# An attention block fused with a rational-function layer: second layer one tick later, another shifted unit, x requested behind its last reader

## The chip, the cores and the metric

One core of a Trainium2 chip runs the whole program. The metric is the device time of one execution in microseconds, less is better. The engines named here are TensorE (PE, with its weight loads as PEld), VectorE (DVE), ScalarE (ACT), GpSimd (POOL), and SyncE (SP), whose queue issues all the DMAs of this program.

## What is computed

`x` has 4 batches of 12480 rows of 128; `inducing` has 32 rows of 128. Cut to what matters:

```python
def mab(q, kv):
    s = scale * (q @ kv.transpose(0, 2, 1))
    a = np.exp(s - s.max(-1, keepdims=True))
    a /= a.sum(-1, keepdims=True) + 1e-09
    return a @ kv
h = mab(I, x)                 # 32 pooled rows of each batch
x2 = mab(x, h)                # each row of x attends to the 32 pooled rows
hh = x2.reshape(49920, 128) @ w_in            # 2048 columns
P = a[0] + a[1] * hh + a[2] * hh**2 + a[3] * hh**3
Q = 1.0 + abs(b[0]) * abs(hh) + abs(b[1]) * hh**2
out = (P / (Q + 1e-6)) @ w_out
```

## The kernel before

**Blocks, units, ticks.** The 49920 rows are cut into 104 blocks of 480 rows (26 per batch). For one block the 2048 hidden columns are worked on in 8 units of 256 (2 halves of 128). So there are 832 units, and `fast_ticks` (L894) writes the program tick by tick: in tick t unit t enters the first layer, and older units are at later stages. Ticks are only a way of writing; on the chip every engine runs its own list in order and waits by semaphores. With t counted from 0 and eight units to a block, the unit number within a block is the tick's number modulo 8, and ticks are named by it below (tick 5 is the tick in which a unit 5 enters).

**What a tick writes.** `first` (L838) for the unit of the next tick: two matmuls into a PSUM tile `hp` (three of them) from the attention weights `at` and the stack `st`. A *plain* unit then gets its absolute value by a bit mask on DVE (`mask`, `u<-hp`) and after that two more matmuls on PE that add a constant to `hp` (`moved`, L853, `hp<-same,by`), which may not start before the mask has read `hp`. A *shifted* unit (`shifted`, L778) has the constant in `st` already, gets its absolute value from ACT and needs neither mask nor `moved`. Units 1, 3 and 7 are shifted, and 0, 2, 4, 5, 6 plain. One tick later DVE forms `l` from `u` and `hp` (`l<-u,all,hp`). ACT turns `u` of pairs of units into a logarithm and later a sigmoid, four pairs at a time. BEHIND = 13 ticks after entering, in odd ticks, DVE finishes the even unit of a pair (`l<-l,all,u`) and POOL the odd one (`last_on_pool`, L952). `second` (L858) multiplies the finished unit with `w_out` into the one PSUM tile `po` of its block: four matmul instructions, two for each half. This happens 14 ticks after entering (`done`, L909), half of it ahead of `first` and half behind; for unit 7 two matmuls (`po<-at,st`) follow that close the block's sum.

**Where a block's result leaves.** `po` exists once. When unit 7 has been through `second`, the next call of `fetch` (L879) writes the copy `oT<-po` on DVE and the DMA of `oT` to the output. `side` (L789), which runs in every tick, calls it (L799), so the copy stands in the same tick behind `l`. The first `second` of the next block may not write `po` before that copy has read it; in its tick, called `late` (L912), `second` therefore stands at the tick's end. With 14 ticks unit 7's `second` falls in tick 5 and the late tick is tick 6.

**Attention beside it.** `side` also feeds the attention work of the next batch and block into the ticks, in small pieces, under a budget of DVE, POOL and PE time per tick (`SPARE`, L195). `pass1` (L375) multiplies x with `inducing` (`pc`, from tiles `xTa`), `pooled` (L446) the exponentials with x (`ph`, from tiles `x`), `pass3` (L651) x with the pooled rows (`pd`, from `xTb`); groups of four blocks of x each, tile by tile in four buffers of a kind. `landed` (L327) holds a group back until three ticks after the request of its fourth tile, where that request has been written already. `columns` (L333) requests tile n+4 when tile n+1 is taken; `pooled` requests tile n+3 at the first reading of tile n. Spreading a block's `at` onto partitions takes eight DMAs from SP per pair of blocks.

Every engine call goes through one helper, so nearly all instructions carry line 177 in the profile; they are told apart by tile names.

Of the kernel before, what the change touches and what calls it, by code (L numbers as in the profile page):

```python
# [21 lines left out]
M = 32  # L22
C = 128
HB = 4
BT = HB * TP
# [167 lines left out]
class Kernel:  # L193
# [138 lines left out]

    def columns(self, b, kind):  # L333

        ts = [self.x_columns(b, n, kind) for n in range(4)]

        def turns():
            for n in range(self.NB):
                yield ts.pop(0)
                if n + 4 < self.NB:  # L340
                    ts.append(self.x_columns(b, n + 4, kind))

        return turns()

    def wide_columns(self, b):

# [28 lines left out]
    def pass1(self, b):  # L375

        nc, ap = self.nc, self.ap
        X = mybir.AxisListType.X
        e = ap.tile([P, self.NG, BT], F32, tag="e", name=f"e{b}")
        mxs = ap.tile([P, self.NG, 2], F32, tag="mxs", name=f"mxs{b}")  # L380
        nc.gpsimd.memset(mxs, -3.0e38)
        xs = self.wide_columns(b) if self.boot else self.cols.pop((b, "a"))
        for g in range(self.NG):
            nb = min(4, self.NB - 4 * g)
            yield from self.landed("a", b, g)
            yield "pe", 1.0
            pc = self.misc(f"pc{b}_{g}")
            for j in range(nb):
                nc.tensor.matmul(pc[M * j:M * j + M, 0:BT], self.ind, next(xs), start=True, stop=True)
            rows = slice(0, M * nb)  # L390
            for i in range(2):
                yield "v", 0.36
                c = slice(BT // 2 * i, BT // 2 * (i + 1))
                nc.vector.tensor_scalar(out=e[rows, g, c], in0=pc[rows, c], scalar1=1.0, scalar2=None, op0=ALU.mult, op1=ALU.max, accum_out=mxs[rows, g, i:i + 1])
            self.free()
        if self.boot:
            self.wide_rows(b)
        else:
            self.xs[b] = [self.x_rows(b, n) for n in range(4)]
        yield "v", 0.1  # L400
        mx = ap.tile([P, 1], F32, tag="mx", name=f"mx{b}")
        nc.vector.tensor_reduce(out=mx, in_=mxs.rearrange("p g i -> p (g i)"), axis=X, op=ALU.max)
        yield "pe", 0.2
        pm = self.misc(f"pm{b}")
        nc.tensor.transpose(out=pm[0:1, 0:P], in_=mx, identity=self.ident)
        yield "v", 0.3
        mt = ap.tile([1, 1, M], F32, tag="mt", name=f"mt{b}")
        nc.vector.tensor_reduce(out=mt[:, 0], in_=pm[0:1, 0:P].rearrange("o (j m) -> o m j", m=M), axis=X, op=ALU.max)
        self.free()
        nm = ap.tile([1, 4, M], F32, tag="H", name=f"nm{b}")  # L410
        nc.vector.tensor_scalar(out=nm, in0=mt.broadcast_to((1, 4, M)), scalar1=-1.0 / math.sqrt(C), scalar2=None, op0=ALU.mult)
        yield "pe", 0.2
        pb = self.misc(f"pb{b}")
        nc.tensor.matmul(pb[:, 0:4], nm.rearrange("o j m -> o (j m)"), self.ones, start=True, stop=True)
        yield "v", 0.1
        nmc = ap.tile([P, 1], F32, tag="nmc", name=f"nmc{b}")
        nc.vector.tensor_copy(out=nmc, in_=pb[:, 0:1])
        self.free()
        self.e[b] = e
        self.exps.append(lambda: self.exp_rows(b, e, nmc))  # L420
        self.flush()
# [24 lines left out]
    def pooled(self, b, own=None):  # L446

        nc, ap = self.nc, self.ap
        e = self.e[b]
        acc = ap.tile([P, C + 1], F32, tag="acc", name=f"acc{b}")  # L450
        xs = self.xs.pop(b)

        def turned(g):
            rows = slice(0, M * min(4, self.NB - 4 * g))
            for c in range(HB):
                yield "pe", 0.22
                if c == 0:
                    pt = self.misc(f"pt{b}_{g}").rearrange("p (c n) -> p c n", c=HB)
                nc.tensor.transpose(out=pt[0:TP, c, rows], in_=e[rows, g, TP * c:TP * c + TP], identity=self.ident[rows, rows])
            eT = ap.tile([TP, HB, P], F32, tag="eT", name=f"eT{b}_{g}", bufs=2)  # L460
            yield from self.act(lambda: nc.scalar.activation(eT[:, :, rows], pt[0:TP, :, rows], AF.Identity, bias=0.0, scale=1.0))
            eTs.append(eT)

        eTs, early = [], int(self.boot)
        while self.e_done.get(b, 0) < self.NG:
            self.flush()
            yield "wait", 0
        if early:
            yield from turned(0)
        for g in range(self.NG):  # L470
            nb = min(4, self.NB - 4 * g)
            if g + early < self.NG:
                yield from turned(g + early)
            eT = eTs.pop(0)
            self.free()
            yield from self.landed("x", b, g)
            for k in range(HB * nb):
                j, c = divmod(k, HB)
                if c == 0:
                    yield "pe", 0.4  # L480
                if k == 0:
                    ph = self.misc(f"ph{b}_{g}")
                if c == 0 and self.boot and (4 * g + j) % 3 == 0 and g + j:
                    self.xs[b] = xs
                    self.wide_rows(b)
                elif c == 0 and not self.boot and 0 < 4 * g + j < self.NB - 3:
                    xs.append(self.x_rows(b, 4 * g + j + 3))
                nc.tensor.matmul(ph[M * c:M * c + M, 0:C + 1], eT[:, c, M * j:M * j + M], xs[4 * g + j][:, c, :], start=(j == 0), stop=(j == nb - 1))
            yield "v", 0.2
            if g == 0:  # L490
                nc.vector.tensor_copy(out=acc, in_=ph[:, 0:C + 1])
            else:
                nc.vector.tensor_tensor(out=acc, in0=ph[:, 0:C + 1], in1=acc, op=ALU.add)
            self.free()
        yield "pe", 0.3
        pq = self.misc(f"pq{b}")
        nc.tensor.matmul(pq[0:M, 0:C + 1], self.fold, acc, start=True, stop=True)
        yield "v", 0.4
        rs = ap.tile([M, 1], F32, tag="rs", name=f"rs{b}")
        nc.vector.tensor_scalar(out=rs, in0=pq[0:M, C:C + 1], scalar1=1e-9, scalar2=None, op0=ALU.add)  # L500
        nc.vector.reciprocal(out=rs, in_=rs)
        yield "v", 0.2
        H = ap.tile([M, C], F32, tag="H", name=f"H{b}")
        nc.vector.tensor_scalar(out=H, in0=pq[0:M, 0:C], scalar1=rs, scalar2=None, op0=ALU.mult)
        self.free()
        yield "pe", 0.3
        pt = self.misc(f"HT{b}")
        nc.tensor.matmul(pt[:, 0:4 * M], H, self.ident4.rearrange("p a m -> p (a m)"), start=True, stop=True)
        yield "v", 0.2
        while own is None and self.scored < b - 2:  # L510
            yield "wait", 0
        HT = own if own is not None else ap.tile([C, 4 * M], F32, tag="HT", name=f"HT{b}", bufs=2)
        nc.vector.tensor_copy(out=HT, in_=pt[:, 0:4 * M])
        self.free()
        self.HT[b] = HT
# [135 lines left out]
    def pass3(self, b, groups):  # L651
# [4 lines left out]
        for fours in groups:  # L656
            wide = ap.tile([TP, 2, HB, 4, M], F32, tag="a", name=f"a{b}_{fours[0]}")
            todo = []
            for i, r in enumerate(fours):
# [3 lines left out]
                for j in range(HB * nb):  # L663
# [1 line left out]
                    if j == 0:  # L665
                        pc = self.misc(f"pd{b}_{r}")
                    if j % HB == 0:
                        xT = next(self.cols[b, "b"])
                    nc.tensor.matmul(pc[0:TP, M * j:M * j + M], xT[:, TP * (j % HB):TP * (j % HB) + TP], self.HT[b][:, 0:M], start=True, stop=True)
                a = wide[:, i, :, 0:nb]  # L670
                sc = pc[0:TP, 0:HB * nb * M].rearrange("p (j c m) -> p j c m", m=M, c=HB)
                yield "v", 0.7
# [104 lines left out]

    def shifted(self, q):  # L778

        return self.fast and q % 2 == 1 and q != 5  # L780

    def step(self, which):

# [110 lines left out]
    def fast_ticks(self, units):  # L894
# [10 lines left out]
            V.tensor_scalar(out=u.u.bitcast(I32), in0=u.h.bitcast(I32), scalar1=0x7FFFFFFF, scalar2=None, op0=ALU.bitwise_and)  # L905

        self.first(units[0])
        for t in range(n + BEHIND + 2):
            u, last, d, done = at(t), at(t - 1), at(t - BEHIND), at(t - BEHIND - 1)  # L909
            group, turn = divmod(t - TURNS - 2, 2 * TURNS)  # L910
            w = at(2 * TURNS * group + 2 * (turn % TURNS))
            late = done and done.key[2] == 0  # L912
# [6 lines left out]
            if u:  # L919
                if t % 2 == 0:  # L920
                    u.pair = self.mp.tile([P, 2, 2, BT], F32, tag="u", name=f"u{u.i}", bufs=self.rooms["u"])
                    u.u = u.pair[:, 0]
                    mask(u)
                    if late:
                        self.fetched = self.fetch()
                else:
                    u.u = last.pair[:, 1]
                    if not plain(u):
                        A.activation(u.u, u.h, AF.Abs, bias=p.z_back, scale=1.0)
            if t % 2 and d:  # L930
                V.scalar_tensor_tensor(out=d.g, in0=d.g, scalar=p.z_k3, in1=d.u, op0=ALU.add, op1=ALU.mult)
                self.last_on_pool(at(t - BEHIND + 1), d)
# [11 lines left out]
                A.activation(w.pair, w.pair, AF.Sigmoid, bias=p.lnc, scale=-2.0)  # L944
            self.side(u or units[-1])
            if late:
                if not u:
                    self.fetch()
                self.second(done)
        self.fetch()  # L950

# [123 lines left out]
                self.again()  # L1075


class Unit:


# [26 lines left out]
```

## Time and profile before

| what | value |
|---|---|
| median of 3 runs | 2566.98 us (2561.35 to 2567.44) |
| profiled execution, its own time | 2566.77 us |
| its span, first to last instruction | 2564.9 us |
| mean granted TensorE clock | 0.956 |
| PE busy | 2285.1 us, 89% |
| DVE busy | 2269.3 us, 88% |
| ACT busy | 2149.7 us, 84% |
| POOL busy | 1445.7 us, 56% |
| DMA | 121.03 MB, mean 47 GB/s |

Shares of busy time are means over the whole span. The first 118 us or so set things up; the ticks fill the rest, and in the last quarter hardly any attention work is left. Three engines are nearly full at once, so an idle stretch on one of them is of interest when another engine waits for what it did not do. A wait in brackets in a timeline is idle time of that engine just before the instruction, with the engine that ended it.

### The profile page before, as it was taken

To read this page: it belongs to the slowest core of one execution; us is meant where nothing else is said; L and a number is where in the kernel's file an instruction comes from. 1 tells how busy PE (TensorE), PEld (TensorE's weight loads), DVE (VectorE), ACT (ScalarE), POOL (GpSimd) and SP (SyncE) were. 2 spreads that over 40 slices of the span, in tenths; PEclk is the share of its full clock that TensorE was granted. 3 is DMA by queue.
4 is the path that set the end of the run, shared out by engine and by line. 5 is a ranking of instruction groups with operands and counts; after the bars stand their busy time and mean duration, and the time that the engine had idled before them with its cause. 6 is when DMAs were issued, how large, how long until landed. Compare 5 with 4: busy or idle time off the path is not lost.

```text
span 2564.9 us, 25969 instructions
## 1 busy us (share of the span) xinstructions
PE 2285.1 (89%) x8670; PEld 1112.6 (43%) x8670; DVE 2269.3 (88%) x2490; ACT 2149.7 (84%) x1487; POOL 1445.7 (56%) x997
## 2 busy tenths in 40 slices
PE   4479999899899899999889989999999999999997
PEld 2244444444434444444434434444444444444443
DVE  2688899889998988988798879999999999999995
ACT  1177899888888998988799968889989899999995
POOL 0325566555555565665465546565656566666666
PEclk6579999999999999999999989999999999999999
DMA  9113201310132012002211220001010100000000
GB/s 251 53 31 115 64 26 31 78 50 20 58 100 62 18 52 66 28 27 89 81 35 35 70 58 27 12 20 43 24 43 23 44 18 30 18 18 20 16 16 17
DMA packets 117112, 121.03 MB, mean 47 GB/s; under 512 B 13289, under 2 KB 115561, under 8 KB 116969
## 3 DMA queue, kind: packets, MB, share of 16 engines
q1 hardware_dynamic: 116969, 119.28, 16.4%
q8 instruction: 70, 1.15, 0.2%
q14 instruction: 73, 0.60, 0.1%
HBM read 80.89 MB, written 25.56 MB: 42 GB/s over the span
## 4 chain that ended last, share of the span: by engine, by line
PE 44%; DVE 33%; issue 11%; ACT 6%; DMA 3%; POOL 2%; SPq 1%; DVEq 0%; POOLq 0%; ACTq 0%
PE po L177 27%; DVE l L177 15%; DVE u L177 12%; PE hp L177 10%; ACT u L177 4%; PE pd L177 3%; DVE oT L177 2%; ACT L177 1%; DVE asm L177 1%; PE pc L177 1%; SPq L177 1%; POOL u L177 1%; DMA xw<-x_t 1%; DMA xTw<-x_c 1%; DVE cv L177 1%
## 5 line engine op out<-in xcount | busy, mean ns | idle before, releaser
L177 PE MATMUL po<-l,w_out 128*128 128x480 f32 x3328 | 1579.4, 580 | 9.0 <-POOL l L177 8.1
L177 DVE SCALAR_TENSOR_TENSOR l<-u,all,hp 128x960 f32<-128x960 f32 x832 | 1002.2, 1205 | 32.8 <-PE hp L177 21.8
L177 POOL TENSOR_SCALAR u<-l,all 128x960 f32<-128x960 f32 x416 | 447.3, 1075 | 958.9 <-DVE l L177 838.7
L177 POOL TENSOR_TENSOR l<-u 128x960 f32<-128x960 f32 x416 | 927.0, 2228 | 34.6
L177 PEld LDWEIGHTS po<-l,w_out 128*128 128x128 f32 x3328 | 628.9, 193 | 380.9 <-issue 213.2
L177 ACT ACTIVATE u<-u,all 128x1920 f32<-128x1920 f32 x416 | 765.3, 1887 | 1.2
L177 ACT ACTIVATE u<-u 128x1920 f32<-128x1920 f32 x416 | 737.5, 1797 | 5.6 <-DVE l L177 4.5
L177 DVE TENSOR_SCALAR u<-hp 128x960 int32<-128x960 int32 x520 | 597.2, 1148 | 99.1 <-PE hp L177 97.2
L177 ACT ACTIVATE u<-hp,all 128x960 f32<-128x960 f32 x312 | 328.0, 1051 | 263.2 <-PE hp L177 257.3
L177 DVE SCALAR_TENSOR_TENSOR l<-l,all,u 128x960 f32<-128x960 f32 x416 | 521.1, 1253 | 2.4 <-ACT u L177 2.4
L177 PE MATMUL hp<-at,st 128*128 128x480 f16 x1664 | 481.0, 371 | 21.3 <-DVE l L177 17.5
L177 PE MATMUL hp<-same,by 96*128 96x480 f16 x1040 | 302.3, 372 | 140.0 <-DVE u L177 134.0
L177 PEld LDWEIGHTS <-st 128*128 128x128 f16 x1872 | 183.0, 99 | 490.1 <-issue 475.1
L177 ACT ACT_TABLE_LOAD x235 | 301.5, 1283 | 4.8 <-PEq L1100 0.7
L177 PEld LDWEIGHTS <-by 96*128 96x128 f16 x1040 | 102.6, 99 | 369.9 <-issue 333.4
L177 DVE COPY oT<-po 128x480 f32<-128x480 f32 x104 | 67.8, 651 | 61.3 <-PE po L177 61.1
L177 PEld LDWEIGHTS pd<-HT,xTb 128*120 128x120 f32 x832 | 101.9, 195 | 17.0 <-issue 9.7
L177 PE MATMUL pd<-HT,xTb 128*120 128x32 f32 x832 | 98.7, 274 | 3.9 <-DMA xTb<-x_c 3.8
L177 PE MATMUL po<-at,st 128*128 128x480 f16 x208 | 59.1, 366 | 0.0
L177 DVE TENSOR_SCALAR_CACHE_REDUCE e<-pc 128x240 f32<-128x240 f32 (+1 forms) x56 | 21.1, 401 | 31.9 <-PE pc L177 31.9
L177 ACT ACTIVATE a<-a 120x512 f32<-120x512 f32 (+2 forms) x21 | 14.9, 728 | 41.1 <-DVE a L177 41.0
L177 PE MATMUL ph<-x,eT 120*32 120x129 f32 x624 | 25.6, 292 | 24.0 <-DMA x<-x_t 14.0
(110 smaller groups left out, 609.4 us busy)
## 6 DMA issues: line engine op xcount, KB each, us to landing
xTb<-x_c SPq DMA_DIRECT2D x104, 240.0 KB, 2.8
out<-oT SPq DMA_DIRECT2D x104, 240.0 KB, 2.0
xTa<-x_c SPq DMA_DIRECT2D x78, 240.0 KB, 3.0
x<-x_t SPq DMA_DIRECT2D x78, 240.0 KB, 4.0
at<-hl SPq DMA_DIRECT2D x416, 30.0 KB, 1.8
xw<-x_t SPq DMA_DIRECT2D x8, 720.0 KB, 13.1
xTw<-x_c SPq DMA_DIRECT2D x5, 960.0 KB, 12.4
raw<-w_in SPq DMA_DIRECT2D x4, 480.0 KB, 10.3
```

The lines of the kernel that those rows point to most:

```text
L177: ins = call(*args, **kw)
```

## The change

`done` moves from 14 to 15 ticks behind (the loop gets one tick more at its end), and the shifted units are 1, 5 and 7 where they were 1, 3 and 7: unit 3 is now masked, unit 5 not. Requests for x move: `columns` returns an object whose `read()` requests tile n+4 right behind the last matmul that reads tile n, and `pooled` requests tile n+4 behind the last matmul of tile n instead of n+3 at the first matmul of tile n. A `fetch` stands in the late tick for every unit, where `side` has already done the copy.

```diff
     def columns(self, b, kind):
-        ts = [self.x_columns(b, n, kind) for n in range(4)]
-        def turns():
-            for n in range(self.NB):
-                yield ts.pop(0)
-                if n + 4 < self.NB:
-                    ts.append(self.x_columns(b, n + 4, kind))
-        return turns()
+        return Blocks([self.x_columns(b, n, kind) for n in range(4)], (self.x_columns(b, n, kind) for n in range(4, self.NB)))
...
-        xs = self.wide_columns(b) if self.boot else self.cols.pop((b, "a"))
+        xs = Blocks([], self.wide_columns(b), ahead=False) if self.boot else self.cols.pop((b, "a"))
...
-                nc.tensor.matmul(pc[M * j:M * j + M, 0:BT], self.ind, next(xs), start=True, stop=True)
+                nc.tensor.matmul(pc[M * j:M * j + M, 0:BT], self.ind, xs.take(), start=True, stop=True)
+                xs.read()
...
-                elif c == 0 and not self.boot and 0 < 4 * g + j < self.NB - 3:
-                    xs.append(self.x_rows(b, 4 * g + j + 3))
                 nc.tensor.matmul(ph[M * c:M * c + M, 0:C + 1], eT[:, c, M * j:M * j + M], xs[4 * g + j][:, c, :], start=(j == 0), stop=(j == nb - 1))
+                if c == HB - 1 and not self.boot and 4 * g + j + 4 < self.NB:
+                    xs.append(self.x_rows(b, 4 * g + j + 4))
...
-                        xT = next(self.cols[b, "b"])
+                        xT = self.cols[b, "b"].take()
                     nc.tensor.matmul(pc[0:TP, M * j:M * j + M], xT[:, TP * (j % HB):TP * (j % HB) + TP], self.HT[b][:, 0:M], start=True, stop=True)
+                    if j % HB == HB - 1:
+                        self.cols[b, "b"].read()
...
     def shifted(self, q):
-        return self.fast and q % 2 == 1 and q != 5
+        return self.fast and q % 2 == 1 and q != 3
...
-        for t in range(n + BEHIND + 2):
-            u, last, d, done = at(t), at(t - 1), at(t - BEHIND), at(t - BEHIND - 1)
+        for t in range(n + BEHIND + 3):
+            u, last, d, done = at(t), at(t - 1), at(t - BEHIND), at(t - BEHIND - 2)
...
-                    if late:
-                        self.fetched = self.fetch()
...
+            if late:
+                self.fetched = self.fetch()
...
-                if not u:
-                    self.fetch()
...
+class Blocks:
+    def __init__(self, held, more, ahead=True):
+        self.held, self.more, self.ahead = held, more, ahead
+    def take(self):
+        return self.held.pop(0) if self.held else next(self.more)
+    def read(self):
+        if self.ahead:
+            self.held += [t for t in [next(self.more, None)] if t is not None]
```

Three places show how instructions move. Names read tile, batch, block, unit and a running number. The first is DVE's list in block 20 of batch 3. Before, from unit 4's mask on:

```order
L177 TENSOR_SCALAR u3_20_4_13902<-hp3_20_4_13886 128x960
L177 SCALAR_TENSOR_TENSOR l3_20_3_13904<-u3_20_2_13878,all_207,hp3_20_3_13874 128x960
L177 SCALAR_TENSOR_TENSOR l3_19_0_13757<-l3_19_0_13757,all_207,u3_19_0_13741 128x960
L177 TENSOR_SCALAR u3_20_4_13902<-hp3_20_5_13898 128x960
L177 SCALAR_TENSOR_TENSOR l3_20_4_13920<-u3_20_4_13902,all_207,hp3_20_4_13886 128x960
L177 COPY oT3_18_13925<-po3_18_0_13834 128x480
L177 TENSOR_SCALAR u3_20_6_13931<-hp3_20_6_13910 128x960
L177 SCALAR_TENSOR_TENSOR l3_20_5_13933<-u3_20_4_13902,all_207,hp3_20_5_13898 128x960
```

Now, from unit 3's mask on:

```order
L177 TENSOR_SCALAR u3_20_2_13876<-hp3_20_3_13872 128x960
L177 SCALAR_TENSOR_TENSOR l3_20_2_13892<-u3_20_2_13876,all_207,hp3_20_2_13860 128x960
L177 TENSOR_SCALAR u3_20_4_13902<-hp3_20_4_13884 128x960
L177 SCALAR_TENSOR_TENSOR l3_20_3_13904<-u3_20_2_13876,all_207,hp3_20_3_13872 128x960
L177 SCALAR_TENSOR_TENSOR l3_19_0_13755<-l3_19_0_13755,all_207,u3_19_0_13739 128x960
L177 SCALAR_TENSOR_TENSOR l3_20_4_13918<-u3_20_4_13902,all_207,hp3_20_4_13884 128x960
L177 TENSOR_SCALAR u3_20_6_13928<-hp3_20_6_13910 128x960
L177 SCALAR_TENSOR_TENSOR l3_20_5_13930<-u3_20_4_13902,all_207,hp3_20_5_13898 128x960
L177 COPY oT3_18_13935<-po3_18_0_13844 128x480
L177 SCALAR_TENSOR_TENSOR l3_19_2_13779<-l3_19_2_13779,all_207,u3_19_2_13763 128x960
```

The second mask of an odd tick has gone from unit 5 to unit 3, and the copy of `po` from behind unit 4's `l`, where a finishing `l<-l`, a mask and an `l` stood ahead of it, to behind unit 5's `l`, where a mask and an `l` do.

The second is PE's list from the two matmuls that close `po` of block 18 on; weight loads are left out, and of pairs of like matmuls the second. Before:

```order
L177 MATMUL po3_18_0_13834<-at3_4_1_13373,st_3_9164 128x480
L177 MATMUL hp3_20_5_13898<-same_701,by_700 128x480
L177 MATMUL hp3_20_7_13928<-at3_5_0_13598,st_3_9164 128x480
L177 MATMUL hp3_20_6_13910<-same_701,by_700 128x480
L177 MATMUL po3_19_0_13938<-l3_19_0_13757,w_out_97 128x480 x2
L177 MATMUL po3_19_0_13938<-l3_19_1_13767,w_out_97 128x480
```

Now:

```order
L177 MATMUL po3_18_0_13844<-at3_4_1_13383,st_3_9578 128x480
L177 MATMUL hp3_20_6_13910<-same_703,by_702 128x480
L177 MATMUL hp3_21_0_13938<-at3_5_0_13608,st_3_9578 128x480
L177 MATMUL po3_19_0_13948<-l3_19_0_13755,w_out_97 128x480 x2
L177 MATMUL po3_19_0_13948<-l3_19_1_13765,w_out_97 128x480
L177 MATMUL hp3_21_1_13952<-at3_5_0_13608,st_3_9578 128x480
```

Before, the late tick had to pass unit 6's `moved` (which follows unit 6's mask, which follows the copy on DVE) ahead of the next block's `po`; now the late tick's own unit 7 is shifted and has none.

The third is SP's list around the second group of `pass1` in batch 1. Before:

```order
L177 DMA xTa1_4_1204<-x_c 128x480
L177 DMA xTa1_5_1207<-x_c 128x480
L177 DMA xTa1_6_1210<-x_c 128x480
L177 DMA out<-oT0_1_1229 128x480
L177 DMA at0_1_1_1232<-hl0_1_1076 32x480 x8
L177 DMA xTa1_7_1281<-x_c 128x480
L177 DMA xTa1_8_1284<-x_c 128x480
```

Now:

```order
L177 DMA xTa1_4_1206<-x_c 128x480
L177 DMA xTa1_5_1209<-x_c 128x480
L177 DMA xTa1_6_1212<-x_c 128x480
L177 DMA xTa1_7_1215<-x_c 128x480
L177 DMA out<-oT0_1_1245 128x480
L177 DMA at0_1_1_1258<-hl0_1_1071 32x480 x8
L177 DMA xTa1_8_1284<-x_c 128x480
```

The fourth tile of the group was requested behind the output and the eight DMAs of `at`, and now stands ahead of them.

## Rows read from the trace of the kernel before

**Rows 1.** Busy time of each engine in four stretches of the program behind its start: per engine, busy us and (x) instructions; then the granted TensorE clock as a share, DMA share, GB/s.

```profile
60.00:700.00 640.00, 545.33 (x2187) 277.39 (x2188) 557.41 (x667) 490.23 (x349) 325.51 (x245) 0.91 0.19 54
700.00:1300.00 600.00, 552.48 (x2146) 264.91 (x2143) 531.59 (x584) 509.74 (x353) 339.28 (x239) 0.97 0.20 59
1300.00:1900.00 600.00, 548.38 (x2095) 269.56 (x2094) 543.91 (x543) 530.42 (x365) 352.44 (x238) 0.97 0.13 36
1900.00:2530.00 630.00, 586.33 (x1944) 278.45 (x1943) 615.49 (x575) 601.76 (x405) 403.48 (x248) 1.00 0.07 22
```

**Rows 2.** Timeline of VectorE (DVE) in one block of the last stretch, which holds no attention work: start us, duration us, engine, operation, out<-in, count, and in brackets the idle time before it and who ended it. The block's unit 5 is worked on from 2418.31 on, its unit 6 from 2422.33 on, and 2427.02 is unit 0 of the next block.

```profile
2418.31 1.34 DVE L177 SCALAR_TENSOR_TENSOR l<-l,all,u 128x960 f32<-128x960 f32 x1
2419.57 1.15 DVE L177 TENSOR_SCALAR u<-hp 128x960 int32<-128x960 int32 x1
2420.64 1.20 DVE L177 SCALAR_TENSOR_TENSOR l<-u,all,hp 128x960 f32<-128x960 f32 x1
2421.76 0.65 DVE L177 COPY oT<-po 128x480 f32<-128x480 f32 x1
2422.33 1.14 DVE L177 TENSOR_SCALAR u<-hp 128x960 int32<-128x960 int32 x1
2423.40 1.20 DVE L177 SCALAR_TENSOR_TENSOR l<-u,all,hp 128x960 f32<-128x960 f32 x1
...
2427.02 1.16 DVE L177 TENSOR_SCALAR u<-hp 128x960 int32<-128x960 int32 x1 [0.17 <-PE hp L177]
```

**Rows 3.** Timeline of TensorE (PE) in the same block, same columns.

```profile
2420.94 0.57 PE L177 MATMUL po<-at,st 128*128 128x480 f16 x2
2421.35 0.57 PE L177 MATMUL hp<-same,by 96*128 96x480 f16 x2
2421.89 0.56 PE L177 MATMUL hp<-at,st 128*128 128x480 f16 x2
2423.53 0.56 PE L177 MATMUL hp<-same,by 96*128 96x480 f16 x2 [1.07 <-DVE u L177]
2423.93 2.58 PE L177 MATMUL po<-l,w_out 128*128 128x480 f32 x6
```

**Rows 4.** Who waited for whom from 60 to 1900 us: engine and tile that waited, what for, us in total, times, longest us.

```profile
DVE u L177 <- PE hp L177: 89.2, 90, 5.1
...
DVE oT L177 <- PE po L177: 38.1, 31, 3.6
...
DVE l L177 <- PE hp L177: 20.7, 34, 2.3
...
DVE l L177 <- ACT u L177: 10.1, 8, 2.0
...
DVE e L177 <- PE pc L177: 9.1, 4, 8.0
...
PE hp L177 <- DVE u L177: 95.6, 88, 3.6
...
PE ph L177 <- DMA x<-x_t: 14.0, 3, 9.6
...
PE pc L177 <- DMA xTa<-x_c: 10.7, 2, 7.7
...
PE ph L177 <- POOL x L177: 10.0, 8, 2.3
...
PE pd L177 <- DMA xTb<-x_c: 3.8, 3, 1.4
```

**Rows 5.** Timeline of SyncE's queue (SPq, which issues every DMA) from 1226 to 1242 us.

```profile
1230.33 4.94 SPq L177 DMA_DIRECT2D at<-hl  x8
1235.32 1.53 SPq L177 DMA_DIRECT2D xTa<-x_c  x3
```

**Rows 6.** Timeline of TensorE in that stretch.

```profile
1229.55 1.01 PE L177 MATMUL pc<-xTa,ind 128*32 128x480 f32 x6
1238.30 1.81 PE L177 MATMUL pc<-xTa,ind 128*32 128x480 f32 x2 [7.74 <-DMA xTa<-x_c]
```

**Rows 7.** Timeline of all engines from 1500 to 1531 us, the rows of the x loads of the pooling pass.

```profile
1520.64 4.94 SPq L177 DMA_DIRECT2D at<-hl  x8
...
1525.69 1.58 SPq L177 DMA_DIRECT2D x<-x_t  x3
...
1529.64 0.66 PE L177 MATMUL ph<-x,eT 120*32 120x129 f32 x8 [9.57 <-DMA x<-x_t]
```

**Rows 8.** Busy time of each engine in four short stretches, columns as in the first group.

```profile
776.00:780.00 4.00, 2.92 (x23) 2.43 (x23) 3.94 (x5) 3.86 (x4) 1.30 (x3) 1.00 0.90 285
780.00:784.00 4.00, 4.00 (x7) 1.46 (x6) 0.58 (x1) 1.74 (x2) 2.18 (x1) 0.57 0.29 84
1524.00:1530.00 6.00, 0.36 (x8) 0.23 (x8) 0.00 (x0) 0.00 (x0) 0.00 (x0) 0.54 0.50 130
1530.00:1534.00 4.00, 4.00 (x15) 1.78 (x8) 2.63 (x3) 2.69 (x3) 2.04 (x2) 0.50 0.09 20
```

**Rows 9.** Who waited for whom from 2410 to 2490 us, four blocks without attention work.

```profile
PE hp L177 <- DVE u L177: 4.3, 4, 1.1
...
DVE u L177 <- PE hp L177: 0.7, 4, 0.2
```

**Rows 10.** What SyncE's queue waited for in the whole program.

```profile
SPq L177 <- PE pd L177: 262.4, 61, 41.4
```

## The prediction

> **What bounds the kernel now.** I read first the busy times by stretch. In the three stretches from 60 to 1900 us DVE is busy 557.4 + 531.6 + 543.9 = 1633 of 1840 us and PE 1646, while from 1900 us on DVE is busy 615.5 of 630 [rows 1]. So there are two regimes. In the last one DVE is full and at most 15 us can be had; before it DVE and PE carry nearly the same load and each stands idle for some 200 us. Then the waits from 60 to 1900 us, to see for what: DVE waits 89.2 + 20.7 us for `hp` and 38.1 us in 31 cases for the `po` that it copies; PE waits 95.6 us in 88 cases, 1.09 us each, for DVE's mask, and 38.5 us for x in its four forms (14.0 + 10.7 + 10.0 + 3.8) [rows 4]. The two wait for each other. Where, a quiet block shows: PE closes `po` at 2420.94, does unit 5's `moved` and unit 7's `first`, and then stands 1.07 us for unit 6's mask [rows 3]. DVE reaches that mask late because tick 5 is its heaviest: finishing `l`, mask, `l` and copy run from 2418.31 to 2422.33 before the mask can start [rows 2]. Only then does PE get to the next block's `po`. In a quiet block that costs DVE 0.17 us at the next unit 0 [rows 2], since DVE is the fuller engine. Any attention matmul in tick 6 is added to it.
>
> The waits for x come from SP's list. At 1230.33 eight `at` requests take SP 4.94 us, and the tile that PE's running group needs is asked for only behind them; PE stands 7.74 us [rows 5, 6]. At 1520.64 the same, and PE stands 9.57 us [rows 7].
>
> **Part by part.**
>
> *Requests for x.* The fourth tile of a group was asked for inside that group; `landed` found no such request and let the group start. Now it is asked for behind the last reader of the tile four earlier, in the group before, and `landed` waits three ticks for it. A tick is about 2.9 us (2412 us for 832), so three are 8.7 us, against the 4.94 + 1.53 us that SP needed for the burst and the three tiles behind it [rows 5]. I count the two long stalls whole, 7.7 + 9.6 us, since DVE stood too (8.0 us for the first [rows 4]), and a quarter of the other 21.2 us, which are short: **-23 us**, bounds -38 and 0. The groups held back cost nothing: by the changed list the preparation of batch 3 ends in tick 529 instead of 506, and is needed in tick 623. The cover is these 94 ticks; for batch 1 it is thin (its first `hl` in tick 194, its first use in 207).
>
> *The late tick and the second odd mask.* Between closing `po` and writing the next one, PE used to need copy and mask from DVE. Now it needs the copy alone, because unit 7, which enters in the late tick, is shifted. From the rows: PE closes at 2420.94, a pair takes 0.57 us, so the copy could start at 2421.51 and end at 2422.16; PE's two pairs behind it keep it until about 2422.17 (three steps of 0.41) [rows 2, 3]. With a passing of 0.06 to 0.1 us each way (mask ends 2423.47, PE goes on 2423.53), the wait falls from 1.07 to 0.2 at most: 0.9 us of PE time per block. Four quiet blocks fill 80 us and hold four such waits [rows 9]; at 20 to 21 us each, the 630 us of the last stretch are 30 blocks, so 74 lie before it. 74 x 0.9 = 67 us of PE time. It is worth time only where DVE or ACT then waits for PE less. DVE waits 110 us for `hp` there, but some of those blocks are full on DVE; I take two thirds, 44 us. In the 30 last blocks DVE can gain no more than its 0.17 us each, 5 us. Together **-49 us**, bounds -72 and 0.
>
> *Clock.* Granted 0.97 over 1200 us [rows 1] means 72 us at the lower of two levels (1.2 GHz), so 36 us of PE work lost. One such stretch follows a PE that was busy 2.92 of 4 us: at 780 us the clock is 0.57 and DVE is left with 0.58 busy of 4 us; another follows the x stall, with 0.50 from 1530 on [rows 8]. PE standing less should keep more of it; I take a third, **-12 us**, bounds -36 and 0. The Trainium skill ("TensorE: Matmul & The Clock Gate", Part 1) says that the clock is halved after a stretch in which the array was idle and comes back with sustained work; by that alone only the two long stalls would be repaid, and the term would be about -8 instead of -12. The row at 776 us speaks for more, since PE was not idle there.
>
> *The copy stands closer to what it waits for.* It needs the closing pair of PE's tick. Before, DVE had a finishing `l`, a mask and an `l` ahead of it in that tick (2418.31 to 2421.76, 3.45 us); now a mask and an `l` (2422.33 to about 2424.5, 2.19 us) [rows 2]. So DVE's cover shrinks by 1.26 us. If only the 31 blocks that wait now wait longer, and PE comes 0.9 us earlier in them, that is 31 x 0.36 = **+11 us**. Bounds: 0, and 74 x 1.26 = 93.
>
> *The rest, at nothing.* Counts of masks, `moved` and absolute values stay the same. The finishing `l` and POOL's product get one more tick before `second` reads them, and PE hardly waits for them. The sixteen `l` buffers are held a tick longer, which DVE can notice only if it outruns PE by two ticks, and its mask already waits for a later matmul of PE. ACT has absolute values in ticks 5, 7, 1 instead of 1, 3, 7, beside a table load; DVE waited for ACT 10.1 us [rows 4], so this bounds to +10. The extra tick at the end holds only matmuls that earlier results release: 0 to +3. The moved `fetch` finds nothing left to do.
>
> Sum: -23 - 49 - 12 + 11 = **-73 us**. The profiled execution took 2566.8 us, as good as the median of 2567.0 (its span, 2564.9, and 1.9 around it). Forecast: **2494 us**.
>
> **Rivals.**
> 1. *Waits change place.* PE's 0.9 us per block is lost again, because attention pieces fall elsewhere and DVE, PE and ACT, all near 90%, collide in other ticks. Only the x term stays: 2544 us. For it: in the quiet blocks nearly all of PE's wait is free. Chance 0.17.
> 2. *The copy becomes the bound, slower.* In the blocks with attention work PE lags, so that DVE stands at the copy in tick 6 in each of them, 93 us, and PE's returned time only shortens that wait: 2567 - 23 + 93 = 2637; if half as bad and nothing is gained elsewhere, 2590. It decides when PE's closing pair ends more than 2.2 us after DVE began unit 6's mask, by 0.3 us in the mean block for no gain at all, by 1 us for more than all the terms. Against it: PE, no longer held in tick 6, starts the next block earlier. Chance 0.08.
> 3. *It does not do what it says.* The requests still land late behind SP's bursts, and PE's wait goes to the copy: 2567, within 8 us. Chance 0.07.
> 4. *All ends far.* x -38, late tick -72, clock -36: 2421 us; near it DVE would be as full as in the last stretch. Chance 0.09.
> 5. *The requests hold SP.* Each of them now waits for a matmul of the same tick, and what stands behind it on SP waits too. SP already waits for `pd` 262.4 us in 61 cases, at the longest 41.4 [rows 10]; with a burst of 4.94 that is 46 us, against 13 ticks, 38 us, from batch 1's first `hl` to its use. Three batch starts at 8.6 us: 2494 + 26 = 2520. Chance 0.04. The Trainium skill ("DMA: Bandwidth & Descriptors", Anatomy of one DMA) says that a wait is made by the issuing sequencer ahead of dispatch, never by the DMA engines; by that rule this rival is what a request behind its reader does to all behind it. Rows 5 and 7 agree as to one list in order.
>
> **The numbers.** The forecast has 0.55, its own range 2466 to 2530 (each term between half and all of its gain, the copy between 0 and 40). A measurement of this kernel can tell about 0.3%, 8 us, from no change. Faster: 0.55 + 0.17 + 0.09 + 0.04 = 0.85; same: rival 3, 0.07; slower: rival 2, 0.08. The range that leaves out no more than 2 in 10 takes in the forecast, rival 5, most of rival 1 and the near part of rival 4: 2440 to 2552.
>
> **What would show it.** Right: PE's waits for DVE's mask from 60 to 1900 us fall from 95.6 to under 30 us; DVE's waits for `hp` from 110 to near 60; its waits for `po` stay at 30 to 60; no PE wait for x over 3 us; quiet blocks at 19.8 us; clock 0.98 or more from 700 to 1900. Wrong: DVE's waits for `po` over 80 us (rival 2), PE's waits for DVE as large as before at another tile (rivals 1 and 3), or PE waiting for `at` near the batch starts (rival 5).

## The result, and the profile after

The changed kernel took **2434.42 us** (median of 4 runs, 2432.16 to 2441.97) against 2564.16 us for the kernel before in 4 runs: a ratio of 0.9503, 95% interval 0.9472 to 0.9535. That is 130 us less, where 73 were forecast; 2434 lies 6 us under the range. The profiled execution took 2433.11 us with a span of 2431.2.

Busy time by stage, the columns as in [rows 1], the last stretch shortened because the program ends earlier:

```profile
60.00:700.00 640.00, 566.31 (x2294) 286.16 (x2295) 582.72 (x744) 524.79 (x372) 351.34 (x259) 0.92 0.20 55
700.00:1300.00 600.00, 579.97 (x2272) 277.85 (x2271) 578.80 (x642) 551.36 (x381) 368.61 (x259) 0.99 0.21 62
1300.00:1900.00 600.00, 579.89 (x2262) 286.92 (x2261) 573.83 (x577) 563.47 (x388) 377.34 (x253) 1.00 0.14 40
1900.00:2400.00 500.00, 482.11 (x1548) 222.14 (x1545) 494.92 (x464) 492.14 (x331) 329.58 (x202) 1.00 0.06 19
```

From 60 to 1900 us PE is busy 1726 us where it was 1646, DVE 1735 where it was 1633, and the clock is 0.99 and 1.00 where it was 0.97 twice. Both engines do 5 to 6% more in the same time. The waits of that stretch, columns as in [rows 4]:

```profile
PE hp L177 <- DVE u L177: 52.4, 71, 4.5
...
DVE oT L177 <- PE po L177: 38.1, 34, 2.3
...
DVE u L177 <- PE hp L177: 22.7, 22, 3.5
...
DVE l L177 <- PE hp L177: 14.1, 12, 2.9
...
DVE acc L177 <- PE ph L177: 2.0, 2, 1.4
...
PE pd L177 <- DMA xTb<-x_c: 1.5, 1, 1.5
...
PE pc L177 <- DMA xTa<-x_c: 0.4, 1, 0.4
```

PE's waits for the mask went from 95.6 to 52.4 us, DVE's for `hp` from 109.9 to 36.8, its waits for `po` stayed at 38.1 us, and the waits for x, 38.5 us in four forms, are 1.9 us. (ph behind the x tiles, which had 14.0 and 10.0 us, is gone from the list.) The changed kernel does five or six more quiet blocks in this stretch. Counted instead over the first 74 blocks of either kernel, all of PE's waits for DVE fell from 111 to 59 us, DVE's for `hp` from 107 to 33, and its waits for `po` went from 38 to 36.

A quiet block, to be laid beside [rows 2] and [rows 3]. DVE first: the copy in tick 6, the finishing `l` of tick 7, then tick 3 of the next block with its finishing `l`, mask and `l`, and the next copy.

```profile
2292.61 0.65 DVE L177 COPY oT<-po 128x480 f32<-128x480 f32 x1
2293.18 1.21 DVE L177 SCALAR_TENSOR_TENSOR l<-l,all,u 128x960 f32<-128x960 f32 x1
...
2302.20 1.33 DVE L177 SCALAR_TENSOR_TENSOR l<-l,all,u 128x960 f32<-128x960 f32 x1
2303.46 1.14 DVE L177 TENSOR_SCALAR u<-hp 128x960 int32<-128x960 int32 x1
2304.53 1.20 DVE L177 SCALAR_TENSOR_TENSOR l<-u,all,hp 128x960 f32<-128x960 f32 x1
...
2312.28 0.65 DVE L177 COPY oT<-po 128x480 f32<-128x480 f32 x1
```

And PE from its closing pair on:

```profile
2291.84 0.57 PE L177 MATMUL po<-at,st 128*128 128x480 f16 x2
2292.24 0.57 PE L177 MATMUL hp<-same,by 96*128 96x480 f16 x2
2292.74 0.56 PE L177 MATMUL hp<-at,st 128*128 128x480 f16 x2
2293.31 2.68 PE L177 MATMUL po<-l,w_out 128*128 128x480 f32 x6
...
2304.66 0.57 PE L177 MATMUL hp<-same,by 96*128 96x480 f16 x2 [0.59 <-DVE u L177]
```

PE closes `po` at 2291.84, does unit 6's `moved` and the next unit 0's `first` and goes on to the next block's `po` at 2293.31, 1.47 us after it began to close; before, that took from 2420.94 to 2423.93, 2.99 us, with the wait of 1.07 us and one pair of matmuls more in between. PE's wait has moved to unit 3's `moved`, 0.59 us at 2304.66, behind the mask that now stands in tick 3. From copy to copy the block takes 19.67 us, and DVE has no gap in it; most quiet blocks of the kernel before took 19.92 us.

### The profile page after: what moved, and what is told of

Same layout as the page of the kernel before. It is cut to its first block, busy times and chain, and to the rows that moved or that the text cites. A ratio compares the mean times of both kernels' runs of the same rounds, so it can differ in the third digit from the quotient of the medians.

```text
span 2431.2 us, 26076 instructions
## 1 busy us (share of the span) xinstructions
PE 2257.5 (93%) x8670; PEld 1093.7 (45%) x8670; DVE 2247.8 (92%) x2490; ACT 2146.2 (88%) x1486; POOL 1449.1 (60%) x997
## 4 chain that ended last, share of the span: by engine, by line
DVE 37%; PE 35%; issue 15%; ACT 7%; DMA 3%; POOL 2%; SPq 2%; DVEq 0%; POOLq 0%; ACTq 0%
PE po L177 20%; DVE l L177 18%; DVE u L177 13%; PE hp L177 8%; ACT u L177 5%; PE pd L177 3%; SPq L177 2%; ACT L177 1%; DVE oT L177 1%; DVE asm L177 1%; DMA xTw<-x_c 1%; DVE cv L177 1%; PE ph L177 1%; PE pl L177 1%; PE pgt L177 1%
## 5 line engine op out<-in xcount | busy, mean ns | idle before, releaser
L177 PEld LDWEIGHTS po<-l,w_out 128*128 128x128 f32 x3328 | 615.8, 191 | 355.7 <-issue 183.2
L177 DVE SCALAR_TENSOR_TENSOR l<-l,all,u 128x960 f32<-128x960 f32 x416 | 527.7, 1269 | 2.3 <-ACT u L177 2.3
L177 PEld LDWEIGHTS <-st 128*128 128x128 f16 (+1 forms) x1872 | 181.8, 98 | 482.2 <-issue 466.6
L177 ACT ACTIVATE e<-e,nmc 128x960 f32<-128x960 f32 (+1 forms) x16 | 15.6, 992 | 31.7 <-DVE nmc L177 31.5
```

The costliest lines, as they stand in the source:

```text
L177: ins = call(*args, **kw)
```

## Experiments

Medians of one job stand beside the kernel before in the same job (2567.8, 2567.4 and 2567.5 us in the three jobs; the change stands beside 2564.2 us in a fourth, so that a difference from it is one between jobs, and is told by the ratios too). In the table "late tick" means 15 ticks with units 1, 5, 7 shifted.

| label | late tick | x requests | groups held | us | ratio to before, 95% |
|---|---|---|---|---|---|
| e1_x_only | no | early | yes | 2514.9 | 0.9793 (0.9752 to 0.9834) |
| e9_x_unheld | no | early | no | 2514.3 | 0.9797 (0.9769 to 0.9825) |
| e2_pace | no | late | yes | 2607.5 | 1.0165 (1.0135 to 1.0194) |
| e3_late_shift | yes | late | no | 2521.3 | 0.9825 (0.9796 to 0.9854) |
| e11_after_pace | yes | late | yes | 2513.7 | 0.9789 (0.9764 to 0.9814) |
| e10_after_unheld | yes | early | no | 2442.8 | 0.9513 (0.9489 to 0.9538) |
| the change | yes | early | yes | 2434.4 | 0.9503 (0.9472 to 0.9535) |
| e4_ticks15 | 15 ticks, 1 3 7 | late | no | 2530.0 | 0.9850 (0.9824 to 0.9877) |
| e12_after_plain5 | 15 ticks, 1 3 7 | early | yes | 2449.2 | 0.9537 (0.9513 to 0.9562) |
| e5_shift3 | 14 ticks, 1 5 7 | late | no | 2573.4 | 1.0020 (1.0003 to 1.0038) |
| e6_fill | no, PE's wait filled | late | no | 2555.2 | 0.9957 (0.9941 to 0.9973) |
| e7_copy_first | yes, copy in tick 7 | early | yes | 2452.2 | 0.9543 (0.9522 to 0.9565) |
| e8_copy_behind | yes, copy behind `l` | early | yes | 2442.6 | 0.9508 (0.9486 to 0.9529) |

### The x requests alone

> The kernel before with the change's x requests alone (14 ticks and units 1, 3, 7 as before). Theory A, the terms of the prediction with the late tick mis-sized: only x stalls go, 20 to 40 us faster than before, and PE's waits for DVE's mask stay at 90 us or more. Rival B, the attention work that is held back and so spread over more ticks is what gained: 60 us or more faster, and PE's waits for the mask fall too.

The edit is the change's `Blocks`, `take`, `read` and the request behind the last reader, on the kernel before. It took 53 us off, more than theory A's 20 to 40 and less than rival B's 60, and PE's waits for the mask stayed:

```profile
PE hp L177 <- DVE u L177: 111.9, 100, 2.5
...
DVE e L177 <- PE pc L177: 0.5, 1, 0.5
```

111.9 us in 100 cases against 95.6 in 88, so theory A holds as to the place and is too small in the price. What the spreading of attention work has in it was asked next, with late requests and the same ticks for the work.

> The kernel before, requests as before, but a group is held until three ticks after the request of its third tile, which spreads the attention work over the same ticks as the change does (the third tile's request is written in the group before). Theory A: 0 to 12 us faster, the long x stalls stay. Rival B: as fast as the run with the x requests alone, within 10 us.

```diff
-        while not self.boot and self.tick < self.issued.get((kind, b, min(4 * g + 3, self.NB - 1)), 0) + 3:
+        while not self.boot and self.tick < self.issued.get((kind, b, min(4 * g + (2 if g else 3), self.NB - 1)), 0) + 3:
```

40 us slower: both theories missed. Holding groups alone makes PE wait longer for x:

```profile
PE pc L177 <- DMA xTa<-x_c: 29.0, 5, 8.5
...
PE ph L177 <- DMA x<-x_t: 27.0, 4, 8.7
...
PE pd L177 <- DMA xTb<-x_c: 8.8, 3, 6.3
...
PE ph L177 <- POOL x L177: 6.3, 5, 2.0
```

71 us, against 38.5. Why late requests cost more when groups are held was not followed further. In the traces DVE, ACT and PE have the same lists here as in the run with the x requests alone. So the 93 us between these two runs come from the place of the requests in SP's list (with the memsets of new x tiles on POOL, which go with them). The other half of the pair keeps the early requests and lets groups go as before:

> The run with the x requests alone, but groups are let go as in the kernel before, so that attention work stands in the same ticks as before and only the requests are earlier. Theory F (the earlier place in SP's list is what removes the stalls): 40 us or more faster than before, PE's waits for x under 8 us. Theory G (request and hold work only together, since without the hold a group starts before its tiles land): 0 to 30 us faster, PE's waits for x 15 us or more.

```diff
-        while not self.boot and self.tick < self.issued.get((kind, b, min(4 * g + 3, self.NB - 1)), 0) + 3:
+        while not self.boot and self.tick < (self.issued.get((kind, b, min(4 * g + 3, self.NB - 1)), 0) if g in (0, self.NG - 1) else 0) + 3:
```

(on the run with the requests alone). 53 us faster, theory F. PE's waits for x are gone without the hold:

```profile
PE hp L177 <- DVE u L177: 101.8, 94, 3.6
...
DVE oT L177 <- PE po L177: 34.0, 30, 3.6
...
PE pd L177 <- DMA xTb<-x_c: 1.5, 1, 1.5
```

With the hold, the same early requests gave 2514.9 us: spreading the work is worth nothing that these runs can tell. In the run without the hold every engine but SP and POOL (the memsets of new x tiles) has the list of the kernel before, and PE finds its tiles landed. So the two traces can be laid side by side block by block (each block from the `l<-u,all,hp` of its unit 0 to that of the next). The 13 blocks of the kernel before in which PE waited over 0.5 us for x are 54.9 us shorter, and all other blocks together 4.5 us. In those 13 blocks PE had waited 37.2 us and in 8 of them the clock had been at its lower level, 41 us in all by the trace's record of granted stretches; in the new run that is 0. The other five have no stretch at the lower clock; PE had waited 7.5 us in them, and they are 9.2 us shorter. So a stall counts whole, short as it may be. A stall with a stretch at the lower clock behind it shows both parts. Here is one of the kernel before, on PE, and the clock behind it (busy times in columns as in [rows 1]):

```profile
482.90 0.43 PE L177 MATMUL ph<-x,eT 120*32 120x129 f32 x8 [3.49 <-DMA x<-x_t]
```

```profile
483.00:487.00 4.00, 4.00 (x16) 1.84 (x16) 2.63 (x3) 2.72 (x3) 2.01 (x2) 0.57 0.83 176
```

PE waited 3.49 us; then the granted clock was 0.57 of full in the mean of 4 us.

### What a stretch at the lower clock costs

> The kernel before with unit 7's first pair of matmuls written twice in the late tick, right ahead of the wait for unit 6's mask: 0.4 us of PE work put into a wait of 1.1 us, with the same result. Theory A (the wait itself is what costs): 0 to 15 us slower. Rival D (the wait costs by way of the clock, which falls when PE stands): 15 to 36 us faster, and the time at the lower clock after 130 us, 118 us before, is halved.

```diff
             if at(t + 1):
                 self.first(at(t + 1))
+                if late and u:
+                    self.first_again(at(t + 1))
```

(`first_again` writes the two matmuls of `first` once more.) 12 us faster, a little under rival D's 15: more PE work made the kernel faster, and theory A's sign was wrong. In the two profiled executions the stretches at the lower clock that begin after 130 us fell from 118 to 63 us in all. That is more than the typical difference, since the one has the lowest clock of its kernel's runs (0.956) and the other the highest (0.972). The median granted clock is 0.959 in fifteen runs of the kernel before and 0.965 in the six of this one, which is about 30 us less at the lower level, or 15 us of PE work. So the runs as a whole bear out about half of what rival D foretold for the clock, and that is enough for the 12 us. A wait of 1 us is not always followed by a fall of the clock: of 61 waits of over 0.9 us ahead of a `moved` in the kernel before (from 190 us to the end of the attention work) 12 were, within 4 us; of 33 in the blocks after it none was, and of the 20 left in the filled run none. The price of one stretch can be read where blocks differ in nothing else. Before, with PE busy 2.93 of 4 us and the clock then at 0.59:

```profile
1780.00:1784.00 4.00, 2.93 (x25) 2.54 (x24) 4.00 (x5) 3.99 (x4) 1.36 (x2) 0.98 0.26 71
1784.00:1788.00 4.00, 4.00 (x8) 1.99 (x9) 0.71 (x1) 2.70 (x2) 2.98 (x2) 0.59 0.37 117
```

The same instructions in the run with early, unheld requests, where the clock stays:

```profile
1722.00:1726.00 4.00, 2.93 (x24) 2.43 (x23) 4.00 (x5) 3.99 (x4) 1.38 (x2) 1.00 0.17 64
1726.00:1730.00 4.00, 4.00 (x17) 2.08 (x15) 1.51 (x2) 2.94 (x2) 3.23 (x2) 1.00 0.44 125
```

PE is busy 2.93 of 4 us in both, yet the clock falls in one run only. PE is busy throughout the next 4 us both times, and DVE gets 1.51 us of work instead of 0.71. From copy to copy that block took, before, in the run with early unheld requests, and in the one with the filled wait:

```profile
1779.62 0.65 DVE L177 COPY oT<-po 128x480 f32<-128x480 f32 x1
...
1807.41 0.65 DVE L177 COPY oT<-po 128x480 f32<-128x480 f32 x1
```

```profile
1721.86 0.65 DVE L177 COPY oT<-po 128x480 f32<-128x480 f32 x1
...
1747.95 0.65 DVE L177 COPY oT<-po 128x480 f32<-128x480 f32 x1
```

```profile
1767.74 0.65 DVE L177 COPY oT<-po 128x480 f32<-128x480 f32 x1
...
1793.85 0.65 DVE L177 COPY oT<-po 128x480 f32<-128x480 f32 x1
```

27.79 us, 26.09 and 26.11: 1.7 us for one stretch of 3.4 us at half clock (by the trace's record), the whole of the PE work lost in it. That is the usual price and not the only one. Between the kernel before and the unheld run nine blocks behind the start-up, without a wait for x, differ by just one such stretch: eight by 1.6 to 1.7 us, one by 2.6. One more block differs by two stretches and again by 1.7 us.

### The late tick alone

> 15 ticks and units 1, 5, 7 shifted, x requests as before. Theory A: 85 to 110 us faster than before, PE's waits for the mask under 60 us from 60 to 1900 us. The prediction's own sizes: 50 us faster. Rival B: under 40 us.

The edit is the change without the x requests. 46 us faster, near the prediction's own 50 and far from theory A's 85 to 110. But it is not the late tick's worth, since the waits for x grew in it:

```profile
PE hp L177 <- DVE u L177: 51.4, 60, 4.4
...
PE pc L177 <- DMA xTa<-x_c: 21.2, 6, 7.6
...
PE ph L177 <- POOL x L177: 14.5, 7, 4.9
...
PE ph L177 <- DMA x<-x_t: 12.1, 2, 8.6
...
PE pd L177 <- DMA xTb<-x_c: 5.5, 4, 2.1
```

53.3 us of waits for x against 38.5; that faster ticks leave the same requests less time is the likely reason, not a tested one. With the requests early in both, the late tick is worth more:

> The changed kernel, but groups are let go as in the kernel before. Theory F: within 15 us of the changed kernel. Theory G: 30 to 70 us slower than it, with PE's waits for x back at 15 us or more.

Same edit to `landed` as above, on the changed kernel. 2442.8 us: theory F. Against the run with early unheld requests without the late tick (2514.3, same job) that is 71.5 us for the late tick. Its waits, to be laid beside 101.8 and 34.0 us in that run:

```profile
PE hp L177 <- DVE u L177: 53.7, 66, 4.5
...
DVE oT L177 <- PE po L177: 42.8, 40, 2.5
```

Against the changed kernel it is 8 us slower by medians of different jobs, with intervals of the ratio that overlap; so the hold adds nothing that these runs tell for certain. DVE, ACT and PE have the same lists here as in the run with the late tick and late requests (2521.3): 79 us for the place of the requests.

> 15 ticks, units 1, 5, 7 shifted, x requests as before, groups held until three ticks after the third tile's request, which puts the attention work into the changed kernel's ticks. If a hold with late requests costs here what it cost on the kernel before (40 us): 2540 to 2575 us. If the late tick's slack absorbs the stalls: under 2510.

The hold of the second experiment on the run with the late tick alone. 2513.7 us lies between the two stated cases, so both missed: with the late tick the hold cost nothing. PE still waits for x, and the same lists of DVE, ACT and PE with early requests are the changed kernel, 79 us faster by medians, 73 by the ratios.

### Ticks, units and the copy

> 15 ticks alone, units 1, 3, 7 shifted and x as before. Theory A, that what counts is that the late tick has no masked unit: within 15 us of the run with 15 ticks and units 1, 5, 7. Rival C, that the even spacing of DVE's heavy ticks (3 and 6 where they were 5 and 5) counts as much: less than half of that run's gain.

Edit: `at(t - BEHIND - 2)` and the loop's end, with `shifted` as before. 38 us faster against 46: theory A. With early requests the same difference:

> The changed kernel with units 1, 3, 7 shifted as before, so that unit 5 is masked and 3 is not: 15 ticks and x requests alone. If the choice of the unit is worth what it was without the x requests (8.6 us): 0 to 15 us slower than the changed kernel. Rival C, spacing of DVE's heavy ticks, which the x stalls covered up: 20 us or more slower.

15 us slower than the change by the medians, at the edge of the first case, 9 by the ratios, whose intervals overlap, and 6 us slower than the changed kernel without the hold, in the same job. The choice of the unit is worth some 6 to 15 us; rival C's spacing carries no more than that.

> Units 1, 5, 7 shifted alone, 14 ticks and x as before. Theory A: the late tick is still tick 6, whose unit is masked, and unit 5's two matmuls no longer lie between PE's closing pair and that wait, so PE's wait for the mask grows from 1.1 to about 1.5 us per block: 0 to 30 us slower than before. Rival C, spacing: 20 us or more faster.

Edit: `q != 5` to `q != 3` alone. 6 us slower, just clear of no change (1.0003 at the least). PE's waits for the mask grew from 95.6 us in 88 cases to

```profile
PE hp L177 <- DVE u L177: 121.8, 98, 4.6
```

1.24 us each instead of 1.09. Alone the other shifted unit is a small loss, as theory A said; it is the late tick's unit that matters.

> The changed kernel with the copy of po written at the start of DVE's tick 7 instead of in tick 6, so that attention pieces of tick 6 stand ahead of it. Theory A: DVE's waits for po fall from 38 us to 20 to 30, time within 10 us of the changed kernel.

```diff
-        if self.fetch() or self.fetched:
+        if not self.hold and self.fetch() or self.fetched:
```

(with `hold` set in the tick whose `second` closes a block, so that the copy is written by the late tick's `fetch`). DVE's waits for `po` fell to 22.7 us, as stated. The time is 18 us above the change by the medians, beyond the 10 us stated, and 10 by the ratios, whose intervals overlap.

> The changed kernel with the copy of po behind the finishing l of tick 7, which gives DVE back the cover that the change took (1.1 us). Theory A: DVE's waits for po fall from 38 us to under 10, but PE now waits for the copy ahead of the next block's po, up to 0.9 us per block where no attention work covers it: 0 to 40 us slower than the changed kernel. Rival E, that the copy's wait is a cost of the change that can be had back: 20 to 38 us faster than it.

As above, with the late `fetch` moved below the finishing `l`. 8 us slower by the medians, the ratio to before the same within its interval. DVE's wait for `po` is gone, and PE waits instead:

```profile
PE po L177 <- DVE oT L177: 47.8, 50, 3.4
...
DVE oT L177 <- PE po L177: 0.8, 3, 0.3
```

47.8 us on PE for 38.1 on DVE. So the wait for the copy is no cost that can be had back in this way; rival E falls.

## Why the prediction missed

**Requests for x: the step that failed.** It counted "a quarter of the other 21.2 us, which are short" and took -23, with -38 as the far end. Measured alone: -53. The short stalls counted whole, and behind most stalls came a stretch at the lower clock: of 54.9 us in 13 blocks 37.2 were stalls, and the other 17.7 are a little under half of the 41 us that these blocks spent at the lower clock. The mechanism (SP's order, the fourth tile behind the `at` burst) was right, and removing its place in SP's list was enough; the hold by `landed` was not needed for it.

**Late tick: right mechanism, small in size.** It took two thirds of 67 us in the first 74 blocks, and 5 us in the last 30. With x out of the way the late tick with its unit brought 71.5 us; the prediction's late tick and copy together are -38. Laid side by side, the first 74 blocks of those two runs differ by 52 us, with 50 us less of PE's waits for DVE (114.7 and 64.4). So the 67 us of PE time were too many, but what there was came back about whole, and the discount for blocks that are full on DVE was not borne out. The last 29 blocks differ by 16 us, and by 14 in the two other pairs of runs with and without the late tick: the limit of 0.17 us to a block did not hold. The wait for the mask did not go to under 30 us as foretold. Of the 95.6 us of the kernel before 66.9 stood at unit 6, and 4.8 do now, but 27.1 came in at unit 3's mask; there it costs DVE nothing in a quiet block.

**Clock: a size too small, and counted in the wrong place.** A third of 36 us was taken as a term by itself. It belongs to the stalls and waits that cause it. In the profiled executions the stretches at the lower clock that begin after 130 us were 118 us before and 45 after, 36 us of PE work. By the median granted clock (0.959 in fifteen runs, 0.968 in the four of the change) it is 27 us, where 12 were counted. Most of it came with the x requests: 0.967 with them alone and unheld, against 0.959 in the same job, is 21 us of PE work, part of the 53 us above. The late tick with late requests gave nothing back (0.958, against 0.961 in its job), with early ones a little (0.970, against 0.967). The rule of the Trainium skill ("TensorE: Matmul & The Clock Gate", Part 1), taken as only the two long idle stretches being repaid, gave -8; the filled wait shows that waits of about 1 us cost clock too, though only some of them.

**Copy: the wait was sized about right, but other gains hid it.** +11 was taken, 93 the bound and the slower rival's price. DVE's waits for `po` are 38.1 us in both kernels, but two things cancel there. With x requests alike on both sides the late tick made them grow: from 34.0 to 42.8 us without the hold, from 31.6 to 38.1 with it, from 38.1 to 46.4 with late requests; counted over the first 74 blocks alone that is 5 to 8 us. The early requests took off about as much. What the longer waits cost in time no run shows by itself; moving the copy back only moved the wait to PE.

**Rivals.** Waits that change place (1) happened for two fifths of the wait at unit 6, without the loss foretold. The copy as the bound (2) and late requests (3) did not happen; a hold on SP (5) did not either: no wait of PE for `at` is in the list. The time lies between all ends far (4), 2421 us, which it misses by 13 us, and the forecast, which it misses by 60. The forecast's own range, 2466 to 2530, does not follow from its rule: half to all of 23, 49 and 12, with 0 to 40 for the copy, is 2483 to 2565. One thing the prediction did not weigh: the parts depend on each other, since the late tick with late requests gave 46 us and with early ones 71.5. The waits for x that grew by 15 us (38.5 to 53.3) are the larger part of that difference.

## What to carry to other kernels

In this kernel, where two engines carry nearly the same load, a stall was to be counted whole, however short, and with the clock behind it: mostly half of each stretch that TensorE spent at the lower level. Which wait is followed by such a stretch could not be told ahead, so the clock is better compared over several runs than in one trace. An unchanged wait between two kernels can be two changes that cancel. A request belongs as early in the issuing queue's order as its buffer allows, ahead of bursts of other requests. And parts of a change are to be timed in the presence of each other: a stall left in place grew when the rest became faster, and made the other part look a third smaller than it was.

## What the runs showed of the hardware

Adding 0.4 us of matmuls per block to a waiting TensorE made the kernel 12 us faster (ratio 0.9957, 0.9941 to 0.9973). Nothing else in the lists of the engines differed, and the median granted clock of the runs was 0.965 instead of 0.959. A stretch of 3.4 us at half clock mostly cost 1.7 us of the program: within 0.15 us of it in eight of nine blocks that differed by one such stretch.

The place of a few requests in SP's list was worth 53 to 93 us while DVE, ACT and PE kept the same lists of instructions (POOL's memsets of new x tiles moved with the requests): 2567 and 2514 us, 2608 and 2515, 2521 and 2443, 2514 and 2434 (these last two in different jobs).
